# Pooled attention and a four-expert attention layer on one core: tail tokens of a batch, and of two batches, in one transfer each

## The chip, the cores and the metric

The kernel runs on one core of one Trainium2 chip. The metric is the device time of one execution in microseconds (us). Compute engines are PE (TensorE, matrix products into PSUM), ACT (ScalarE), DVE (VectorE) and POOL (GpSimd); SP (SyncE) issues the transfers, which 16 DMA engines carry out. Each engine works through its own instructions in order and waits at semaphores for the others.

## What is computed

The reference first pools k and v over runs of 8 tokens, attends with every q, and feeds the result as x to four attention experts; each token's result is weighted by a softmax over its two best experts.

```python
# q, k, v: (8 batches, 8 heads, 576 tokens, 64)
k_p = k.reshape(B, H, Sp, 8, D).mean(axis=3)          # Sp = 72
v_p = v.reshape(B, H, Sp, 8, D).mean(axis=3)
attn = softmax(q @ k_p^T / 8)
x = (attn @ v_p) as (B, 576, 512)
logits = x @ w_gate                                    # 4 experts, the best 2 kept
for e in range(4):
    q, k, v = x @ wq[e], x @ wk[e], x @ wv[e]          # 64 wide
    a = softmax(causal(q @ k^T / 8))
    out += weight[e] * (a @ v @ wo[e])                 # (B, 576, 512), zero weight if e isn't kept
```

## The kernel before

**Tiling.** A batch has 576 tokens: 512 "main" tokens, four rows of 128, and a tail of 64. The main tokens go batch by batch. Tails of q, x and out go by pairs of batches (b - 1, b) with b odd, 128 rows together (`part_t`, line 742). For k and v each batch's tail is loaded by itself (`load_tail`, line 308): a tile of 128 partitions by 4 heads by 64, whose lower 64 partitions hold the 64 tokens of heads 0 to 3, the upper 64 those of heads 4 to 7, by two transfers.

**Pooling on PE.** Sums over tokens are matrix products with 0 or 1/8 masks. `pm` (line 186) pools main tokens; `pmt` (lines 187 and 188) has two masks for tails: `pmt[0]` takes the lower 64 partitions to pooled tokens 64 to 71, `pmt[1]` the upper 64. `pool_k` (line 349) and `pool_v` (line 365) use mask 0 for heads 0 to 3 and mask 1 for heads 4 to 7.

**An order written out by hand.** The program is cut into units, named batch:unit. `ORDER` (line 21) lists them; a unit that yields stands there once for each of its stages. All instructions that the units issue keep the order of that list on their engine (`in_order`, line 125). The loop at line 955 walks the list. Units that matter here:

- `b:lk`, `b:lq`, `b:lv` load main tokens (`0:` in four parts, `1:` in two), `b:lkt`, `b:lvt`, `b:lqt` the tails, `b:kt` and `b:vt` cast the k and v tails on POOL; `b:kp`, `b:vp` pool.
- `b:q`, `b:s`, `b:a`, `b:x` are q transposed, pooled scores, scores times v, x transposed; `b:xd0` to `b:xd3` do the last by DMA transposes for batches 6 and 7.
- `b:p0` to `b:p3` and `b:v0`, `b:v2` project x; `b:c...` are the experts' scores (PE, then exponentials on ACT, then the causal mask on POOL); `b:o0`, `b:o1` scores times values (PE, then scaling on DVE); `b:t0`, `b:t1` transpose the result (by DMA for batches 4 to 6).
- `b:w0` ... and `b:y0` ... multiply 128 rows by wo: PE, then a copy to an `ofin` buffer, by ACT for w and by DVE for y, then a store of 128 rows on SP. There are four `ofin` buffers.
- `b:qx`, `sx`, `ax`, `xx`, `pt`, `vx`, `h0`, `h1`, `hd`, `ox`, `tx`, `w4` with b odd do the same for a pair's tails. The last, `wo` at line 926, computes 128 rows, copies them to an `ofin` buffer and stores them with two transfers of 64 rows, one for each batch. `7:w4` is the last unit of the kernel.
- `W:lk`, `W:lq`, `W:lv`, `W:lo` load weights, `W:c...` cast them, and `W:h0` to `W:h31` (`busy`, line 274) are fillers: two products of zeros each, which nothing reads.

A store's semaphore releases its `ofin` buffer; the copy that writes the buffer next waits for it.

Of the kernel before, what the change touches and what calls it, by code (L numbers as in the profile page):

```python
# [22 lines left out]
0:lk2 0:qc2a 1:q0 1:q1 0:qc0a W:h29 0:qc0d 1:q1 W:h1 0:lk0 W:h21 0:qc1d 0:qc1a 0:lk3 0:q0 0:lv0 W:h7
W:h3 0:qc3d 0:q0 0:ks2 0:q1 0:lk1 0:q1 0:lv2 W:h8 0:ks3 W:h19 W:h14 0:kp2 0:lvt 0:qc2d 0:lv3 0:ks0
0:q2 0:kp2 0:lv1 0:q2 1:kt W:h6 0:vs2 1:lq1 W:h2 0:kp3 0:ks1 W:h27 0:qc3a W:h18 0:q3 1:lk0 0:kp3
0:q3 0:kp1 0:s2 0:vs0 1:lk1 0:kp1 0:s1 0:vs3 0:vt 0:vs1 0:s3 0:kp0 W:h26 0:kp0 1:lv1 W:h15 0:vp 0:s1
0:s2 1:lvt W:h25 0:vp 1:lv0 W:h22 1:qc1a 0:s3 0:a2 1:qc1d 0:s0 W:h16 W:lk W:h24 0:a3 W:h5 0:lqt 0:a2
1:q2 1:ks0 W:h13 1:ks1 1:kp0 0:a3 1:q2 0:s0 0:a1 1:kp0 0:a0 W:h4 1:kp1 W:h28 1:q3 0:a0 1:kp1 0:a1
W:h17 1:s0 0:x0 1:s0 1:s2 1:q3 1:s3 0:x0 1:s1 W:lq W:lv 1:s2 1:lqt 1:vs1 0:x1 1:s3 2:lq W:h10 W:h9
0:x3 0:x1 1:vt W:h0 W:c1 0:x2 1:vs0 2:lkt 0:x3 2:lk W:c3 0:x2 1:vp 1:vp 0:p1 1:a0 1:a2 1:a2 1:s1  # L30
0:p1 W:c2 W:c0 0:p3 1:a1 1:qt 1:a0 2:qc 2:lv 1:a1 0:p3 0:p2 1:a3 W:cv 0:p0 0:p2 0:v2 0:p0 1:a3 2:kt
3:lqt 1:x2 0:v2 1:qx 0:c10 0:c10 0:c2 0:v0 2:lvt 1:qx 1:x3 1:x2 0:v0 0:c2 1:x0 1:x3 3:lk 0:c11 1:x0
1:sx 1:x1 1:x1 0:c11 0:c11 0:c00 0:c00 0:g1 0:g2 2:q3 2:q3 2:q0 1:sx 1:v2 0:c2 3:lvt 2:q2 0:c01 2:ks
2:lqt 0:c10 3:lkt 1:ax 2:q2 2:q1 2:q0 1:ax 1:p1 1:p1 1:v0 0:c01 2:kp 2:q1 1:v2 1:p2 2:vs 2:kp 0:g3
2:vt 1:v0 1:xx 2:s2 3:lq 1:xx 1:p2 2:s0 2:s1 1:vx 0:g4 2:s2 2:s1 1:vx 2:s0 3:lv 1:g1 2:s3 0:g5 1:g2
2:vp 0:o1 2:vp 2:s3 1:pt 2:a2 0:g6 3:ks 1:pt 3:kt 2:a0 1:p3 4:lq 3:qt 0:c01 0:o1 2:a3 2:a2 0:c00
1:p0 1:g3 2:a0 1:p3 2:a3 2:a1 1:c11 3:qc 3:kp 1:p0 4:lk 3:qx 3:vt 2:a1 1:hd 3:qx 1:c11 1:h0 1:hd
1:c2 3:kp 2:x2 2:x1 1:h0 2:x2 4:lkt 0:o0 2:x1 2:x3 4:lv 4:lvt 2:x0 1:c10 1:c2 1:g4 0:o0 3:sx 2:x3
1:c00 3:q1 2:x0 1:c2 1:c10 1:c00 3:q3 1:h1 3:q1 3:q3 3:q2 3:q0 2:v2 3:vs 1:h1 3:q2 1:c11 4:qc 3:q0
5:lq 0:t0 1:g5 0:t1 2:v0 2:v2 3:sx 3:s3 3:s1 0:t1 3:vp 0:t0 3:s3 2:p1 6:lvt 1:hd 4:ks 3:s1 2:p1 2:v0  # L40
3:s2 4:kt 1:c10 3:s0 3:vp 3:s2 3:a3 2:p0 3:a3 4:q2 3:a1 3:ax 4:q2 3:s0 4:q1 1:c01 2:p0 4:q3 4:q1
2:p3 1:c01 2:p3 5:lqt 2:c01 3:a1 4:q3 4:q0 3:ax 2:c01 3:a0 1:c00 4:q0 4:kp 4:kp 3:a2 3:a0 3:a2 2:p2
3:xx 2:p2 6:lkt 1:g6 4:s2 3:xx 4:s0 4:s0 5:lkt 4:s2 1:ox 3:x3 2:g1 1:c01 4:vt 1:o0 2:c00 4:s1 1:ox
3:x3 3:x1 4:vs 2:g2 2:c00 5:qc 4:vp 3:x1 4:s1 3:pt 4:s3 2:c11 3:pt 4:vp 1:o0 3:x0 3:x2 1:o1 2:c01
3:x0 W:lo 3:x2 5:q2 4:lqt 4:s3 2:c00 5:lk 2:c11 3:p3 5:q2 5:lvt 5:q3 1:o1 5:lv 2:c2 3:p3 2:c10 5:q1
4:a3 5:kt 2:c2 5:q3 2:c10 3:p1 4:a0 5:q1 3:p1 W:co 4:a3 3:p2 3:vx 4:a0 6:lqt 4:a1 3:p2 3:vx 3:v0
4:a1 7:lqt 3:v0 0:w0 2:g3 3:hd 6:lq 3:c10 2:c11 1:t1 4:a2 5:qt 2:g4 5:ks 0:w0 3:p0 1:t1 5:q0 4:a2
3:c10 3:hd 5:q0 5:vt 3:p0 3:h0 2:c2 3:c11 5:qx 5:kp 3:c11 3:v2 5:kp 5:qx 2:g5 0:w3 3:v2 3:h0 2:g6
4:x1 4:x1 5:s3 0:w3 3:g1 5:s1 4:x2 5:vs 1:t0 7:lkt 5:s3 2:c10 2:o0 6:lk 4:x2 0:w2 1:t0 4:x0 6:qc
2:o0 5:sx 5:s1 3:c2 3:c10 6:vt 0:w2 5:sx 5:s0 5:s0 7:kt 6:lv 3:c11 3:g2 4:x0 4:x3 5:vp 4:x3 3:c2  # L50
5:vp 3:hd 2:o1 4:p1 3:c2 2:o1 0:w1 4:p1 6:kt 5:s2 3:h1 0:w1 6:q3 6:q0 5:ax 6:q3 4:p0 6:q0 2:t0 3:h1
6:ks 5:ax 5:s2 3:g3 2:t0 0:w3 7:lvt 4:v2 2:t1 4:p0 6:q1 5:a2 3:g4 2:t1 7:qt 6:vs 5:a0 6:q1 5:a0 1:w3
4:p3 5:a1 1:w3 4:p3 5:a2 4:v2 4:p2 7:lq 5:xx 3:c00 3:c01 4:p2 5:a1 0:w2 6:kp 5:a3 3:c00 7:lk 5:xx
3:c01 6:kp 3:g5 3:g6 7:ks 0:w0 5:pt 6:q2 6:s3 5:a3 4:c01 6:q2 4:c00 5:pt 1:tx 1:tx 6:vp 5:x0 6:s3
4:v0 4:c00 5:x0 6:vp 2:w1 4:c01 4:v0 5:x3 6:s0 4:c2 2:w1 5:x1 5:x3 6:s1 5:x1 0:w1 6:s0 7:qc 6:s1
7:lv 2:w0 5:x2 3:o1 6:a0 5:x2 3:c01 2:w0 1:w4 3:c00 3:o1 5:p3 1:w4 4:c2 7:kp 6:a0 7:kp 4:g1 4:c10
4:c11 6:s2 5:p3 7:vs 4:c11 4:c10 7:q3 1:w4 3:ox 6:s2 7:q3 7:q2 5:v0 4:c10 3:ox 2:w1 6:a3 5:vx 7:q2
5:v0 2:w2 5:vx 6:a2 6:a1 6:a3 6:a2 1:w0 2:w2 1:w0 4:g2 2:w0 5:p2 2:w3 5:p2 5:hd 7:s3 6:a1 1:w0 7:q1
2:w3 5:hd 7:q1 4:c00 7:vt 4:c2 5:hd 5:v2 4:c11 4:g3 1:w2 3:t1 5:h1 7:s3 7:s1 1:w2 5:h1 7:s1 6:xd2
5:v2 2:w3 3:t1 7:vp 5:g1 5:p1 6:xd3 7:s2 4:g4 2:w2 7:vp 5:c10 5:p1 7:a3 7:s2 7:a3 7:q0 7:q0 4:g5  # L60
5:p0 3:o0 5:g2 4:c01 3:o0 7:qx 6:xd0 5:p0 4:o0 1:w1 5:c10 5:c2 7:s0 4:g6 7:qx 6:xd1 1:w1 3:t0 7:s0
6:p3 5:g3 3:t0 3:tx 3:tx 6:v2 6:p3 6:p0 5:c2 7:a1 1:w1 4:o0 7:a0 3:w4 6:v2 4:t0 7:a1 6:p0 1:w2 3:w4
6:p1 7:a2 5:g4 7:a0 3:w2 3:w2 5:h0 7:a2 5:c10 5:g5 7:sx 4:o1 6:p1 4:o1 1:w3 3:y1 3:y1 6:p2 5:c11
7:sx 5:h0 5:g6 5:c01 7:xd0 7:xd1 5:c11 6:p2 5:c01 5:c00 5:ox 6:v0 4:t1 3:w2 3:w3 5:ox 3:w3 3:w0 6:v0
3:w0 5:c01 7:ax 7:v0 7:ax 7:v0 4:w2 5:c11 7:xx 7:xd3 6:c2 5:c2 7:xx 6:g1 5:c00 3:y1 4:w2 6:c00 5:o1
4:w3 6:c2 7:xd2 5:o1 7:vx 3:w3 7:v2 3:w4 6:g2 6:c2 4:w3 7:p2 6:c11 6:c00 6:c10 6:g3 5:c00 7:v2 7:p2
6:c11 7:vx 6:c01 5:t1 7:p3 4:y1 6:g4 7:p3 4:w3 7:g1 4:y1 6:c10 4:y1 5:o0 5:o0 7:g2 6:c01 6:c00 6:g5
4:y0 4:y0 5:t0 7:p0 6:c11 6:c10 6:o1 7:c11 7:p0 6:g6 7:c10 6:c01 7:g3 7:g4 6:o1 4:w2 7:p1 5:tx 6:o0
5:tx 6:o0 7:c10 7:p1 7:c10 3:w0 7:c11 5:w4 5:y1 6:t1 7:g5 7:c2 7:c01 5:w4 7:c2 7:c00 7:c11 5:y1 4:y0
7:g6 5:y2 7:c01 7:pt 7:c2 7:c01 7:pt 5:y2 6:t0 7:c00 5:y1 5:y0 5:y0 7:c00 7:o1 5:w3 7:o1 7:hd 6:y1  # L70
# [919 lines left out]
```

## Time and profile before

| | us |
|---|---|
| three runs | 177.66, 178.21, 178.53 |
| their median | 178.21 |
| the profiled execution | 176.43 |
| its span, first to last instruction | 174.7 |

The span was taken at a granted TensorE clock of 0.996 of full speed. The profile's page gives busy time and shares of the span for each engine, a picture of the span in 40 slices, and the chain of work that ended last, followed back from the last instruction: at each step to what released it, or to the instruction before it on its engine. Rows of groups read: line, engine, operation, out<-in, shapes, how many | busy time, mean ns of one | idle time just before them and what ended it. L133 is the line of the helper that records every ordered instruction, so most rows are told apart by their tiles. Rows of a timeline read: start, length, engine, line, operation, and in brackets the idle time before it with its releaser. SPq is SP's queue of transfers, where the length is that of the issue alone; the rows of DMA issues give KB of one transfer and the median time from issue to landing.

| DMA, 40 slices of 4.37 us | |
|---|---|
| busy share in tenths | 4999999999999999979999999061632866267886 |

Of 42.03 MB in all, 30.42 MB are read from HBM and 9.44 MB written to it. 36 stores leave from `ofin`: 28 of 256 KB and 8 of 128 KB; the last copy into such a buffer starts at 170.3 us and the last issue at 171.4 us.

### The profile page before, as it was taken

What the parts mean: (1) busy time and instruction counts of PE and PEld (TensorE: products, weight loads), DVE (VectorE), ACT (ScalarE), POOL (GpSimd) and SP (SyncE); (2) the same over time, 40 slices, a digit from 0 to 9 for tenths busy, and PEclk for the clock granted to TensorE, in tenths of its full rate; (3) what the DMA queues carried; (4) which work ended last, traced back from release to release, by engine and by line L of the source; (5) the groups of instructions that cost most, each with busy time, mean ns of one, the idle gap of its engine ahead of it and who ended that gap; (6) DMA issues with size and microseconds to landing.
All of it is one profiled execution on the core that took longest, in us unless ns stands there. A gap on an engine that the chain in (4) does not pass through costs nothing.

```text
span 174.7 us, 5295 instructions
## 1 busy us (share of the span) xinstructions
PE 163.1 (93%) x2088; PEld 101.2 (58%) x2088; DVE 123.7 (71%) x354; ACT 125.0 (72%) x176; POOL 101.2 (58%) x227
## 2 busy tenths in 40 slices
PE   7698999999999999999999999999999999989990
PEld 2244454567577745775675757675466586546550
DVE  6456586777688867988877697689678656675760
ACT  2210909876788977789899859896987877888841
POOL 8504333147989999873689995963802054655200
PEclk9999999999999999999999999999999999999998
DMA  4999999999999999979999999061632866267886
GB/s 151 280 337 304 344 296 282 263 325 262 250 221 345 346 281 288 190 209 311 260 284 339 332 365 365 25 177 67 172 72 90 183 181 157 90 135 250 267 332 194
DMA packets 52968, 42.03 MB, mean 241 GB/s; under 512 B 21968, under 2 KB 48080, under 8 KB 52944
## 3 DMA queue, kind: packets, MB, share of 16 engines
q1 hardware_dynamic: 52944, 41.70, 86.4%
q8 instruction: 16, 0.26, 0.7%
q14 instruction: 8, 0.07, 0.1%
HBM read 30.42 MB, written 9.44 MB: 228 GB/s over the span
## 4 chain that ended last, share of the span: by engine, by line
PE 72%; DMA 11%; ACT 8%; DVE 4%; SPq 1%; issue 1%; ACTq 0%; DVEq 0%
PE p_ps L133 15%; PE v_ps L133 7%; PE y_ps L133 6%; PE idle_ps L133 5%; PE sB_ps L133 5%; PE sA_ps L133 4%; PE oA_ps L133 4%; PE qT_ps L133 4%; PE oB_ps L133 4%; PE vp_ps L133 3%; DMA out_dram<-ofin 3%; DMA ktail<-in_k_dram 3%; PE xT_ps L133 3%; DMA kraw<-in_k_dram 3%; PE oBt_ps L133 3%; ACT etA L133 3%
## 5 line engine op out<-in xcount | busy, mean ns | idle before, releaser
L133 ACT ACTIVATE etA<-sA_ps 72x1024 bf16<-72x1024 f32 x32 | 31.4, 1018 | 12.7 <-PE sA_ps L133 12.6
L133 ACT ACTIVATE etB<-sB_ps 128x1024 bf16<-128x1024 f32 x32 | 32.3, 1027 | 3.0 <-PE sB_ps L133 2.7
L133 PE MATMUL p_ps<-xT,wqk 128*128 128x512 bf16 x128 | 32.9, 379 | 0.1
L133 POOL TENSOR_SCALAR_AFFINE_SELECT etB<-etB 128x256 bf16<-128x256 bf16 x48 | 18.5, 407 | 12.0 <-ACT etB L133 11.8
L133 ACT CAST qk<-p_ps 128x512 bf16<-128x512 f32 x32 | 18.8, 587 | 9.2 <-PE p_ps L133 9.0
L133 DVE TENSOR_TENSOR x_tm<-oA_ps,rzA 128x512 bf16<-128x512 f32 x32 | 22.1, 691 | 1.1
L133 POOL TENSOR_TENSOR vsum<-vraw 128x512 bf16<-128x512 f32 (+2 forms) x18 | 18.4, 1043 | 7.5 <-DMA vraw<-in_v_dram 7.5
L133 PE MATMUL idle_ps<-idle 128*128 128x512 bf16 x64 | 19.6, 418 | 1.9 <-DVE idle L160 1.2
L133 PEld LDWEIGHTS <-wqk 128*128 128x128 bf16 x192 | 15.0, 97 | 10.3 <-issue 0.9
L133 POOL TENSOR_TENSOR ksum<-kraw 128x512 bf16<-128x512 f32 (+1 forms) x16 | 17.8, 1134 | 4.8 <-DMA kraw<-in_k_dram 4.6
L133 PE MATMUL y_ps<-wo_t,oT 128*128 128x512 bf16 x64 | 18.4, 379 | 1.0 <-DMA oT<-o_sc 0.7
L133 DVE COPY qT<-qT_ps 128x512 bf16<-128x512 bf16 x32 | 15.2, 486 | 5.8 <-PE qT_ps L133 5.5
L133 ACT COPY ofin<-y_ps 128x512 f32<-128x512 f32 x20 | 11.7, 586 | 10.0 <-PE y_ps L133 6.8
L133 PE MATMUL v_ps<-wvg,xT 128*128 128x260 bf16 x128 | 17.0, 274 | 0.0
L133 PE MATMUL qT_ps<-ident,qbf 128*128 128x128 bf16 x128 | 11.9, 220 | 2.1 <-DVE qbf L133 1.4
L133 PE MATMUL sB_ps<-qk 64*128 64x256 bf16 (+3 forms) x128 | 13.6, 299 | 0.0
L133 DVE COPY xT<-xT_ps 128x512 bf16<-128x512 bf16 x24 | 9.7, 419 | 4.6 <-PE xT_ps L133 4.5
L133 PEld LDWEIGHTS <-xT 128*128 128x128 bf16 x128 | 11.6, 97 | 2.4 <-DVE x_tt L133 0.4
L133 POOL CAST qbf<-qraw 128x2048 bf16<-128x2048 f32 x6 | 11.3, 1889 | 2.8 <-PE sB_ps L133 2.4
L133 PEld LDWEIGHTS <-etA 72*128 72x128 bf16 x256 | 10.6, 97 | 3.9 <-issue 1.0
L133 PEld LDWEIGHTS <-qbf 128*128 128x128 bf16 x128 | 8.3, 97 | 7.4 <-issue 2.7
L133 PEld LDWEIGHTS <-etB 128*128 128x128 bf16 x256 | 11.4, 97 | 1.7 <-POOL etB L133 0.5
(123 smaller groups left out, 333.1 us busy)
## 6 DMA issues: line engine op xcount, KB each, us to landing
out_dram<-ofin SPq DMA_DIRECT2D x28, 256.0 KB, 2.7
qraw<-in_q_dram SPq DMA_DIRECT2D x6, 1024.0 KB, 9.5
...
qraw<-in_q_dram SPq DMA_DIRECT2D x4, 256.0 KB, 4.7
...
ktail<-in_k_dram SPq DMA_DIRECT2D x16, 64.0 KB, 5.7
kraw<-in_k_dram SPq DMA_DIRECT2D x4, 256.0 KB, 4.8
```

The costliest lines, as they stand in the source:

```text
L133: return tc.keep_in_program_order(fn(*args, **kwargs))
```

## The change

Four things change.

1. The tails of k and of v of a batch come in one transfer of 128 KB each. The tile has the same shape, but its rows are laid out otherwise: partition 2t + half holds token t, of heads 0 to 3 for half 0 and of heads 4 to 7 for half 1.
2. The two tail masks follow that layout. POOL makes one mask `pmr`, in which 16 partitions in a row belong to one pooled token; DVE reduces the identity to two columns that say whether a partition is even or odd, and multiplies.
3. `part_t`'s `wo` stores its 128 rows with one transfer for both batches. For the last pair its copy is split in two halves of 256 columns, one on ACT, one on DVE.
4. `ORDER` is a new list of the same units, each the same number of times.

```diff
 ORDER = """
-0:lq0 W:h12 1:lq0 0:lkt W:h20 0:lq2 0:lq3 W:h30 0:kt 1:qc0a W:h23 1:lkt W:h11 1:qc0d 0:lq1 1:q0
...
+0:lq2 W:h30 0:qc2d 0:lq1 W:h16 W:h8 0:qc1a W:h12 0:qc1d W:h9 W:h13 0:lq0 0:qc2a 0:lv0 0:lk3 W:h17
...
+6:p1 5:hd 7:a2 7:a0 5:h0 3:w4 1:w1 5:c2 7:xd1 2:w3 3:t0 4:o1 7:sx 6:p2 3:t0 5:h0 5:c11 6:p2 1:w0
+5:c01 7:xd2 5:c01 4:o1 5:c00 3:y1 5:ox 5:c11 7:ax 4:t1 3:y1 3:w2 5:c00 3:w2 5:c00 7:ax 6:v0 5:c11
+6:v2 5:ox 3:w0 3:w0 6:v0 6:c00 6:v2 6:c2 7:xd3 6:g1 7:xd0 7:xx 4:w3 5:o1 7:xx 6:c00 3:w0 6:g2 7:vx
+5:c01 7:v2 3:w4 7:vx 6:c2 4:w3 3:w2 7:v0 7:v2 4:w2 5:o1 6:g3 4:w2 7:p2 3:y1 7:v0 7:p2 3:w3 6:c10
+6:c11 6:g4 3:w3 6:c01 6:c10 4:y1 7:p3 6:c10 6:c11 4:y1 5:o0 7:p3 7:p0 4:w2 6:c01 4:y0 3:w3 7:c11
+6:c11 7:c10 7:p0 5:o0 6:c00 5:tx 5:t1 4:y1 7:c10 4:y0 6:c2 6:g5 6:c01 6:o1 7:g1 7:c11 5:t0 4:y0 7:p1
+5:tx 6:o0 6:g6 5:w4 7:g2 4:w3 7:p1 7:c2 7:g3 6:o1 5:w4 6:o0 7:c11 6:t1 7:c00 5:y1 5:y2 7:c2 6:t0
+5:y1 7:c10 5:y2 7:c2 7:g4 7:c01 7:pt 5:y0 7:c01 7:c01 5:w4 7:pt 7:o1 7:g5 5:y1 5:w3 7:c00 5:y0 5:w3
+7:g6 7:hd 7:c00 7:o1 6:y1 7:hd 7:o0 6:y1 6:w0 7:t1 7:h1 5:y2 7:h0 7:o0 7:t1 6:w0 7:hd 7:t0 5:w3 6:y3
+7:t0 6:y1 6:w0 7:h1 5:y0 6:y3 7:z2 7:h0 6:w2 6:y3 7:ox 7:z2 7:z0 6:w2 7:ox 7:tx 6:w2 7:tx W:h31 7:z0
+7:w4 7:w4 7:w4
 """
...
-    pmt = [pooling("pmt0", MAIN, POOLW), pooling("pmt1", MAIN - 64, POOLW)]
-    nc.gpsimd.memset(pmt[1][0:64, :], 0.0)
+    rows = pooling("pmr", 2 * MAIN, 2 * POOLW)
+    parity = const.tile([128, 2, 1], BF16, name="parity")
+    nc.vector.tensor_reduce(
+        out=parity[:, :, 0], in_=ident[:, :].rearrange("p (i half) -> p half i", half=2),
+        axis=AX_X, op=MAXOP,
+    )
+    pmt = []
+    for half in range(2):
+        t = const.tile([128, 128], BF16, name=f"pmt{half}")
+        nc.vector.tensor_tensor(
+            out=t[:], in0=rows[:], in1=parity[:, half, :].to_broadcast([128, 128]), op=MULT
+        )
+        pmt.append(t)
...
-            for half in range(2):
-                sp.dma_start(
-                    out=t[half * 64 : half * 64 + 64, :].rearrange("p (h d) -> p h d", h=4),
-                    in_=srcs[nm][b, half * 4 : half * 4 + 4, MAIN:S, :].rearrange("h t d -> t h d"),
-                )
+            sp.dma_start(
+                out=t[:].rearrange("p (h d) -> p h d", h=4),
+                in_=srcs[nm][b, :, MAIN:S, :].rearrange("h t d -> t h d"),
+            )
...
-            copy(out=t[:], in_=ps[:])
-            yield
-            for i, b_ in enumerate(both):
-                store(out[b_, MAIN:S, :], t[i * TAIL : (i + 1) * TAIL, :])
+            if b < B - 1:
+                copy(out=t[:], in_=ps[:])
+            else:
+                for half, eng in ((slice(0, DM // 2), act.copy), (slice(DM // 2, DM), dve.tensor_copy)):
+                    eng(out=t[:, half], in_=ps[:, half])
+            yield
+            store(out[b - 1 : b + 1, MAIN:S, :], t[:])
```

More of the change, by code (lines that the diff above doesn't have):

```diff
@@ L21 @@
 ORDER = """
-0:lq0 W:h12 1:lq0 0:lkt W:h20 0:lq2 0:lq3 W:h30 0:kt 1:qc0a W:h23 1:lkt W:h11 1:qc0d 0:lq1 1:q0
[L23 to L70, printed above, removed]
@@ L71 @@
-7:o0 5:w3 6:w0 5:y2 5:y0 6:y1 7:hd 7:o0 7:h1 7:t1 6:w0 7:h0 7:t0 7:t1 7:t0 7:h1 7:hd 5:w3 5:w4 6:y3
-6:w0 6:y1 6:y3 6:y3 7:h0 7:z2 7:ox 6:w2 7:z2 7:z0 7:ox 7:tx 6:w2 7:tx 6:w2 W:h31 7:w4 7:z0 7:w4 7:w4
+0:lq2 W:h30 0:qc2d 0:lq1 W:h16 W:h8 0:qc1a W:h12 0:qc1d W:h9 W:h13 0:lq0 0:qc2a 0:lv0 0:lk3 W:h17
+W:h2 W:h23 0:ks3 0:q1 0:lq3 W:h6 0:lkt W:h1 0:kt 0:lk1 W:h19 W:h7 0:lv1 0:qc3a 0:vs0 0:lv2 0:lk2
+0:q1 1:lq0 W:h3 0:q2 W:h11 0:q2 0:ks1 W:h15 0:qc0d W:h4 0:lv3 W:h24 0:kp3 0:kp1 0:kp1 0:qc3d 0:ks2
@@ new lines @@
+0:kp2 0:qc0a 0:s1 0:lk0 0:kp2 0:kp3 0:q3 0:q3 0:lvt 1:qc0d 1:lq1 0:q0 1:qc0a W:h20 0:q0 1:lk1 1:q0
+0:s1 0:vs2 0:ks0 0:vs1 W:h29 0:vs3 1:lkt 0:kp0 1:lvt 0:s3 0:s2 1:qc1a 1:lk0 1:q0 0:vt 0:s2 0:kp0
+1:qc1d 0:vp 0:s0 0:vp W:h27 1:q2 1:lv0 1:q2 1:ks1 0:s3 W:h21 0:a1 0:a1 1:lv1 1:q1 1:vt 0:a2 W:lk
+W:h0 0:a3 W:lq W:h5 1:q3 1:q1 W:h25 1:kt 1:ks0 W:h22 W:lv 1:vs0 0:a2 0:lqt W:h14 1:lqt 0:a3 1:kp1
+0:s0 0:a0 1:q3 1:kp1 0:a0 1:kp0 1:s2 1:s3 0:x0 1:kp0 0:x2 0:x0 0:x2 1:s1 1:s2 2:lq 1:s0 W:h10 0:x1
+W:h18 1:s1 2:lk W:h26 1:vs1 1:s0 W:c1 0:x1 0:x3 2:lkt W:c3 1:s3 1:vp 2:lv 0:x3 1:vp 0:p1 W:c0 1:a3
@@ new lines @@
+1:a2 0:p3 2:lvt W:c2 3:lk 1:a0 1:qt 1:a2 0:p1 2:qc 1:a3 0:p3 0:p0 W:cv 1:a0 1:a1 1:a1 0:p2 0:p0 0:v0
+0:p2 1:qx 0:v2 1:x0 2:lqt 1:qx 0:v0 1:x0 0:c11 0:c2 W:h28 1:x1 0:v2 1:x3 0:c2 0:g1 0:c11 1:x1 0:c00
+0:c2 1:sx 1:x2 3:lqt 1:sx 1:x3 0:g2 1:x2 2:q1 0:c00 3:lkt 2:q1 3:lq 0:c10 0:c10 1:p1 1:ax 0:c11
+3:lvt 1:v2 0:g3 2:ks 2:q0 3:lv 4:lq 1:ax 1:v2 0:c01 1:p1 2:q3 2:kt 2:q0 0:g4 2:vs 2:q3 0:g5 1:v0
+2:kp 1:p2 2:vt 2:kp 1:xx 0:c01 4:lk 1:v0 0:g6 4:lkt 0:c10 2:s0 2:s3 1:p2 0:c00 1:xx 2:q2 4:lvt 2:s0
+2:s3 2:q2 1:vx 2:s1 1:vx 2:s2 1:g1 2:vp 2:vp 0:o1 2:s2 2:s1 3:ks 4:lv 1:pt 3:kt 2:a3 2:a1 0:o1 2:a2
@@ new lines @@
+0:c01 2:a3 1:pt 1:p3 2:a1 1:p0 2:a2 1:p3 2:a0 2:a0 1:c11 3:kp 1:p0 3:qt 3:qx 1:g2 1:c11 3:kp 1:hd
+1:h0 3:qx 1:c2 1:hd 1:g3 2:x2 2:x1 0:o0 2:x2 1:h0 2:x1 2:x3 3:qc 0:o0 2:x3 1:c2 2:x0 2:x0 1:c10
+1:c00 3:sx 1:c10 3:q2 3:q3 3:q3 3:sx 3:q2 1:hd 2:v2 1:c00 0:t1 3:s3 3:q1 0:t1 1:c11 2:v2 3:q0 5:lq
+2:v0 3:q1 3:s3 0:t0 3:q0 1:h1 3:vt 3:vs 2:v0 0:t0 3:s1 3:vp 1:h1 3:vp 2:g1 1:g4 5:lk 2:p1 3:s0 3:s2
+3:s1 4:qc 1:c10 3:a3 1:c00 4:ks 3:a3 4:q2 4:q2 2:p1 2:p0 1:c01 3:s0 4:q1 4:kt 3:s2 3:a1 4:vt 2:p0
+3:ax 1:c01 4:q1 1:c01 4:q3 2:p3 2:g2 1:c2 3:a2 3:a1 4:q3 3:ax 4:q0 2:c01 2:p3 4:kp 3:a0 4:q0 1:g5
@@ new lines @@
+2:c01 2:p2 4:kp 2:p2 3:a2 3:xx 4:s0 2:c00 4:lqt 1:ox 1:g6 3:a0 3:xx 3:x1 5:lqt 1:o0 2:c00 4:vs 4:s2
+4:s0 5:lkt 4:s1 1:ox 3:x3 3:x1 4:s2 3:x3 5:qc 4:s1 4:vp 3:pt 3:pt 4:vp 2:c11 2:c11 W:lo 4:s3 6:lkt
+3:x2 1:o0 5:lvt 3:x0 3:x2 1:o1 5:q2 3:x0 3:p3 4:s3 5:q2 5:q3 2:c2 1:o1 3:p3 5:lv 5:q3 2:g3 2:c10
+2:c2 5:q1 4:a3 2:g4 2:c01 3:p2 2:c10 5:qt 5:q1 4:a1 4:a3 3:p2 4:a1 5:ks W:co 3:p1 2:g5 4:a0 2:c10
+3:v0 6:lq 0:w0 3:p1 3:vx 4:a0 0:w0 5:kt 3:hd 2:c2 3:c10 7:lqt 3:v0 4:a2 6:lvt 2:c11 3:vx 2:g6 3:hd
+1:t1 1:t1 3:p0 4:a2 5:q0 3:c10 3:c11 3:p0 3:c11 3:h0 5:q0 2:c00 5:qx 5:qx 5:vs 5:kp 5:kp 3:v2 0:w3
@@ new lines @@
+3:h0 5:vt 4:x1 5:s1 0:w3 3:v2 4:x1 5:s3 1:t0 4:x2 2:o0 6:qc 6:lv 1:t0 6:vt 4:x0 5:s1 4:x2 5:s3 0:w2
+3:c10 5:sx 0:w2 3:c11 2:o0 3:c2 5:sx 5:s0 4:x3 6:lk 4:x0 4:x3 5:vp 7:lkt 0:w1 3:c2 2:o1 5:vp 3:g1
+6:kt 6:q3 0:w2 0:w1 5:s0 5:ax 6:q3 2:o1 3:g2 4:p1 2:t0 3:h1 3:g3 4:p1 7:lk 5:s2 2:t0 6:q0 3:h1 6:q0
+4:p0 6:q1 5:ax 5:s2 6:q1 4:v2 3:hd 2:t1 3:g4 7:kt 4:v2 4:p0 5:a0 5:a2 7:lq 1:w3 5:a1 0:w1 2:t1 5:a0
+5:a2 1:w3 4:p3 4:p2 4:p3 6:ks 6:vs 5:xx 3:c01 5:a1 4:p2 3:c00 6:kp 5:xx 5:a3 5:pt 3:c01 3:c2 3:c00
@@ new lines @@
+6:kp 6:q2 3:g5 6:s3 4:c01 5:pt 6:s3 3:c01 5:a3 4:c00 1:tx 6:q2 6:vp 1:tx 5:x0 4:v0 5:x0 6:vp 2:w1
+4:c01 6:lqt 4:c00 5:x3 6:s1 2:w1 3:g6 7:qc 4:v0 6:s0 5:x3 6:s0 0:w0 5:x2 4:g1 5:x2 6:s1 5:x1 3:o1
+5:x1 1:w4 1:w3 7:lv 1:w4 2:w0 7:ks 6:a0 4:c2 2:w0 3:o1 4:c01 6:s2 6:a0 7:kp 5:p3 7:kp 4:c2 7:q3 0:w3
+5:p3 4:c11 4:c10 7:q3 4:g2 6:s2 7:lvt 2:w0 7:q2 3:ox 7:q2 4:c10 2:w2 6:a1 5:v0 3:ox 2:w2 6:a1 7:vt
+5:v0 5:vx 5:vx 7:qt 6:a3 5:p2 6:a2 1:w0 6:a3 5:hd 4:c11 7:s3 5:p2 6:a2 1:w0 4:c00 2:w3 7:s3 2:w1
+2:w3 7:q1 7:q1 4:c2 1:w4 5:v2 7:vs 6:xd3 1:w2 4:g3 4:g4 3:t1 5:v2 3:c00 4:c11 5:g1 6:xd0 5:hd 7:s1
@@ new lines @@
+1:w2 5:c10 7:s1 3:t1 7:s2 7:s2 7:vp 5:p1 5:h1 7:vp 5:g2 5:p1 6:xd1 7:q0 7:a3 5:p0 6:xd2 7:q0 5:h1
+4:g5 3:tx 7:a3 4:c10 5:p0 3:tx 3:o0 1:w1 7:qx 5:g3 4:o0 5:c10 5:c2 4:g6 3:o0 7:s0 7:qx 4:o0 2:w2
+6:p3 1:w1 7:a1 5:c2 7:s0 5:g4 6:p0 5:c10 5:g5 7:a2 7:a1 7:a0 1:w2 5:g6 6:p3 6:p1 6:p0 3:w4 7:sx 4:t0
+6:p1 5:hd 7:a2 7:a0 5:h0 3:w4 1:w1 5:c2 7:xd1 2:w3 3:t0 4:o1 7:sx 6:p2 3:t0 5:h0 5:c11 6:p2 1:w0
+5:c01 7:xd2 5:c01 4:o1 5:c00 3:y1 5:ox 5:c11 7:ax 4:t1 3:y1 3:w2 5:c00 3:w2 5:c00 7:ax 6:v0 5:c11
+6:v2 5:ox 3:w0 3:w0 6:v0 6:c00 6:v2 6:c2 7:xd3 6:g1 7:xd0 7:xx 4:w3 5:o1 7:xx 6:c00 3:w0 6:g2 7:vx
```

## The prediction

> **What bounds the kernel now.** I read the page first (busy shares, the chain by engine), then a table of stretches, then the end of the chain of waits.
>
> ```profile
> PE 163.1 (93%) x2088; PEld 101.2 (58%) x2088; DVE 123.7 (71%) x354; ACT 125.0 (72%) x176; POOL 101.2 (58%) x227
> PE 72%; DMA 11%; ACT 8%; DVE 4%; SPq 1%; issue 1%; ACTq 0%; DVEq 0%
> ```
> ```profile
> 20.00:30.00 10.00, 9.52 (x96) 4.96 (x95) 7.37 (x18) 5.08 (x7) 4.91 (x7) 1.00 1.13 302
> 31.00:90.00 59.00, 57.92 (x823) 39.13 (x821) 45.75 (x133) 47.70 (x67) 43.76 (x79) 1.00 1.07 275
> 90.00:130.00 40.00, 39.76 (x561) 26.08 (x560) 31.53 (x91) 33.53 (x48) 29.51 (x57) 1.00 0.72 219
> 130.00:170.90 40.90, 38.76 (x522) 23.39 (x518) 27.12 (x79) 31.57 (x47) 14.40 (x47) 1.00 0.64 184
> ```
>
> Columns: stretch, its length, busy time of PE, PEld, DVE, ACT, POOL, granted clock, DMA share, GB/s. Before 31 us the sixteen DMA engines are full (share 1.13) and PE fills its time with filler matmuls; from 31 to 130 us PE is busy 97.7 of 99 us; from 130 us there are holes, 2.1 us in 41. So loads set the time up to 31 us, PE from there, and the end is what follows PE's last matmul:
>
> ```profile
> 159.99 2.23 DMA out_dram<-ofin
> 162.31 0.59 ACT ofin L133
> 162.90 0.27 ACT etD L133
> 164.76 0.40 PE oT_ps L133 x4
> 169.64 0.57 PE yt_ps L133 x2
> 170.28 0.59 ACT ofin L133
> ```
>
> In the last 15 us the chain already runs once through a store: ACT may not copy into an `ofin` buffer until the store that last read it has landed. Landing times of stores are therefore a price on the path, not only at the very end.
>
> **What each part costs.**
>
> *Tail loads of k and v.* 32 issues become 16.
>
> ```profile
> ktail<-in_k_dram SPq DMA_DIRECT2D x16, 64.0 KB, 5.7
> vtail<-in_v_dram SPq DMA_DIRECT2D x16, 64.0 KB, 7.1
> qtail<-in_q_dram SPq DMA_DIRECT2D x8, 128.0 KB, 7.1
> 1.79 1.41 SPq L133 DMA_DIRECT2D ktail<-in_k_dram  x2
> ```
>
> The q tail already moves 128 KB in one transfer and lands in 7.1 us, no later than the v halves. A pair costs SP 1.41 us to issue, one transfer about half. From 0 to 31 us SP is ahead of full DMA engines, afterwards PE hides the loads: 0 to -0.7 us, I take -0.2.
>
> *Masks.* POOL builds one mask fewer (2.35 us for two selects alone), DVE gets a reduce and two products of 128x128, by the nearest row, the 0.25 us copy of `perm`, about 0.8 us.
>
> ```profile
> 2.59 2.35 POOL L176 TENSOR_SCALAR_AFFINE_SELECT pmt<-pmt 128x72 bf16<-128x72 bf16 x2
> 4.48 0.25 DVE L166 COPY perm<-ident 128x128 bf16<-128x128 bf16 x1
> 6.60 0.43 DVE L133 CAST qbf<-qraw 128x512 bf16<-128x512 f32 x1 [1.63 <-DMA qraw<-in_q_dram]
> 12.91 0.20 PE L133 MATMUL kpT_ps<-pmt,ktb 128*128 128x72 bf16 x1
> ```
>
> DVE idles 1.63 us before its first cast, waiting for q, and the masks are first used at 12.91 us: 0. Without that cover it would be 0.8 us.
>
> *Order.* The two orders hold the same units. I counted the PE units that stand ahead of the first projection `0:p1`: the same set in both, except that one filler, `W:h28`, moves from ahead of it to after it. All loads of batches 0 and 1 but their q tails stand ahead of `W:lk` in both, so the DMA-bound start stays. One pair of fillers costs
>
> ```profile
> 22.60 0.59 PE L133 MATMUL idle_ps<-idle 128*128 128x512 bf16 x2
> ```
>
> 0.59 us where PE is full, 0 in a hole: +0.3. What else the order moves I can bound by PE's holes alone: about 3.5 us idle between 31 and 170.9 us (139.9 less the three stretches' 136.4) is all that a perfect order could win; as much could be lost. I take 0 and keep ±1.5.
>
> *Last copy split.* A half copy:
>
> ```profile
> 8.11 0.71 ACT L133 CAST qbf<-qraw 128x256 bf16<-128x256 f32 x2 [0.90 <-DMA qraw<-in_q_dram]
> 168.39 0.42 DVE L133 TENSOR_TENSOR o_st<-oBt_ps,gt 128x256 bf16<-128x256 f32 x1
> ```
>
> 0.36 us on ACT, 0.42 on DVE, side by side, for 0.59: -0.2.
>
> *Joint tail store.* This is the term that decides.
>
> ```profile
> 171.00:172.00 1.00, 0.00 (x0) 0.00 (x0) 0.00 (x0) 0.00 (x0) 0.00 (x0) 1.00 0.97 367
> 172.00:173.00 1.00, 0.00 (x0) 0.00 (x0) 0.00 (x0) 0.00 (x0) 0.00 (x0) 1.00 0.97 217
> ```
> ```profile
> DMA packets 384, 0.66 MB, mean 170 GB/s; under 512 B 64, under 2 KB 64, under 8 KB 384
> q1 hardware_dynamic: 384, 0.66, 58.1%
> out_dram<-ofin SPq DMA_DIRECT2D x2, 128.0 KB, 2.3
> ```
> ```profile
> 170.90 1.11 SPq L133 DMA_DIRECT2D out_dram<-ofin  x2
> out_dram<-ofin SPq DMA_DIRECT2D x28, 256.0 KB, 2.7
> ```
>
> The first two rows are the drain at the end, the next three its DMA from 170.95 us on. A second with 128-row stores moves 367 GB/s, the next, with the two 64-row stores, 217 GB/s, both with the engines 0.97 busy: how a transfer's rows lie sets its rate. At 367 GB/s each of 16 engines moves a 2 KB row in 0.97 x 16 x 2.048 / 367 = 0.087 us. The 64 small packets are 16 for each of four stores that end in this stretch: every store so far ran on all 16 engines. All have 64 or 128 rows outermost on both sides. The joint store does not: its rows in `out` are two runs of 64, one per batch, 576 rows apart, so that side is [2, 64, 512] with 2 outermost.
>
> If it is still spread over 16 engines, a store costs 8 x 0.087 = 0.7 us of engine time, and the pair's second issue (half of 1.11 us) goes too. If it is split along the outermost count, two engines get 64 rows each: 64 x 0.087 = 5.6 us, and it lands 4.9 us later, 2.4 + 4.9 = 7.3 us after its issue. No row of this trace shows a transfer with fewer than 16 in that place. I take two engines: that a transfer's rate goes by its outermost rows is what the 64-row stores show, and an outermost count of 2 gives two parts.
>
> The Trainium skill (DMA: Bandwidth & Descriptors, Why a DMA increments its semaphore by 16 and not by 1) says the engine count is the largest number up to 16 that divides both sides' slowest dimension, here 2. The same page's Rules for kernel authors ask for one 128-partition transfer in place of two halves, which by 367 against 217 GB/s this trace agrees with; by that alone the change would be a gain at the end.
>
> On two engines the four joint stores cost as follows; distances are unit counts of the new order priced by these pieces of the chain and groups:
>
> ```profile
> 146.99 0.45 PE vt_ps L133 x4
> 147.44 0.94 PE v_ps L133 x8
> 149.24 0.76 PE sB_ps L133 x10
> 150.97 0.43 PE y_ps L133 x2
> 151.40 0.61 PE oB_ps L133 x20
> ```
> ```profile
> 158.67 1.22 SPq L133 DMA_TRANSPOSE oT<-o_sc  x1
> 163.57 0.20 DVE L133 RECIPROCAL oB_ps<-oB_ps 128x8 f32<-128x8 f32 x1
> 164.01 0.69 DVE L133 TENSOR_TENSOR o_sc<-oB_ps,gt 128x512 bf16<-128x512 f32 x1
> L133 ACT ACTIVATE etB<-sB_ps 128x1024 bf16<-128x1024 f32 x32 | 32.3, 1027 | 3.0 <-PE sB_ps L133 2.7
> 162.31 0.59 ACT L133 COPY ofin<-y_ps 128x512 f32<-128x512 f32 x1 [0.71 <-DMA out_dram<-ofin]
> ```
>
> Which buffer a copy gets I took as the one whose store was issued first among those free (four `ofin` buffers).
>
> - `1:w4`: the next copy into its buffer is `1:w2`, and SP reaches the store as soon as `2:w0` is copied, two dozen units and, priced by the same pieces, some 12 us of PE earlier: 0.
> - `3:w4`: its store follows `3:w0`'s, so it issues about 1.2 us after that copy starts and lands at 1.2 + 7.3 = 8.5. The buffer's next writer is ACT's `4:w2`, behind 6:c00, 6:c2, 7:xx, 4:w3, 5:o1, 7:vx, 7:v2, 7:v0 and itself: 0.76 + 0.40 + 0.43 + 0.61 + 0.45 + 2 x 0.94 + 0.43 = 5.0 us. ACT waits 3.5 us, and behind it its exponentials. PE has a projection and the second PSUM buffer to go on with; between 0 and 3.5 I take 1.5.
> - `5:w4`: its store stands behind the DMA transposes 6:t1 and 6:t0. The matmuls of 6:o0 end 0.43 us before those of `5:w4`; DVE's scaling takes from 163.57 to 164.70, 1.1 us; 6:t0's issue 1.22 us, and 6:t1's may still run for 0.5: so the store issues some 2.4 us after its own copy starts and lands at 9.7. The buffer's next writer is `5:w3`, with three exponentials and one cast ahead of it on ACT: 0.59 + 3 x 1.03 + 0.59 = 4.3 us. ACT waits 5.4 us, where 0.71 us was waited before, so at most 4.7 more; queued behind it are 7:hd, 7:h1 and 7:h0, which PE needs for its last scores-times-values, so little hides it: +4.0 (the other bound is 0, if other buffers come free first).
> - `7:w4`: nothing is behind it. Its second store issued at 170.90 + 0.55 and landed 2.3 us later, at 173.8; from there to the end of the span are 0.9 us. Now: issue at 170.7 (the split's 0.2 earlier), landing 178.0, end 178.9: +4.2, the split included.
>
> Sum, in the order named: 1.5 + 4.0 + 4.2 for the stores, -0.2 loads, +0.3 filler, 0 masks: +9.8 us on a span of 174.7, to 184.5. The profiled execution took 176.43 us, 1.7 more than its span; the shown runs have a median of 178.21, 1.8 above that. On the median: 188.0.
>
> **Rivals.**
>
> 1. *Two engines, but only the end pays.* The waits at `3:w4` and `5:w4` are taken up by ACT's idle time or another buffer. For it: ACT is busy 31.57 of 40.9 us there. Against it: the chain shows an ACT copy that waited for a store in this very place. 178.2 + 4.2 + 0.1 = 182.5.
> 2. *Sixteen engines* (the other side). The spread does not go by the outermost count of `out`; then the end gains the split (0.2), the second issue (0.5) and the slower drain of the half stores. It decides in the packets: eight 2 KB rows per engine, or 64. 0.2 + 0.5 + 0.2 of loads - 0.3 filler: 177.6; without the filler's cost 177.3.
> 3. *The new order itself loses* on sixteen engines: PE-bound stages run the filler at 0.59 us and get about 1 us more holes than the 3.5 they have, the drain gains nothing, the split and the loads 0.4: 178.2 + 0.6 + 1.0 - 0.4 = 179.4.
>
> **How the numbers follow.** Forecast 0.50, rival 1 0.32, rival 2 0.13, rival 3 0.05. Around the forecast the `3:w4` and `5:w4` terms run from 0 to 3.5 and 0 to 4.7 and the order ±1.5, so 184 to 192; rival 1 with the order's ±1.5 reaches down to 181.0. The range 181.0 to 192.0 leaves out rivals 2 and 3 and a little above. A change under 0.5% (0.9 us) can't be told from none: faster, most of rival 2, 0.10; same, the rest of it and part of rival 3, 0.06; slower 0.84.
>
> **What will show it.** The DMA issues: 256 KB `ofin` stores, four of them landing 7 us after issue (two engines) or 2.4 (sixteen). After the last ACT and DVE half copies, DMA share near 2/16 = 0.125 and some 46 GB/s for over 4 us. A wait of ACT for `out_dram<-ofin` of 3 to 5 us before two copies, with PE idle behind the second. Masks: DVE's first qbf cast not later than 6.6 us. If the last store lands in about 2.4 us, the forecast is wrong at its first step; if it lands in 7 but ACT waits under 1 us, rival 1 holds.

## The result, and the profile after

| | before | after |
|---|---|---|
| median of four runs, us | 178.03 (177.66 to 178.53) | 192.09 (191.14 to 192.52) |
| ratio to before | | 1.078, 95% interval 1.073 to 1.083 |
| profiled execution: span, us | 174.7 | 190.2 |
| granted TensorE clock over the span | 0.996 | 0.943 |

The change costs 14 us; the forecast was 10. The forecast time was 188.0 us in a range of 181.0 to 192.0: 192.09 us lies at the upper end, 0.1 us past it. From the page of the changed kernel, the busy times, the granted clock in 40 slices of 4.75 us, and the row of the 256 KB stores:

```profile
PE 165.0 (87%) x2088; PEld 101.9 (54%) x2088; DVE 123.5 (65%) x358; ACT 124.8 (66%) x176; POOL 100.1 (53%) x222
PEclk9999999999999999999999999999999579975965
out_dram<-ofin SPq DMA_DIRECT2D x32, 256.0 KB, 2.4
```

No engine has more to do (the same 2088 matmuls take 1.9 us more). The median landing time in that row, 2.4 us, says nothing of the four joint stores: the trace has no landing time for them in that row. The table of stretches shows where the time stands, and the first new thing: the clock column (after the five busy times) falls.

```profile
130.00:140.00 10.00, 10.00 (x168) 6.74 (x166) 6.69 (x19) 7.72 (x11) 1.69 (x5) 1.00 0.70 147
140.00:150.00 10.00, 5.75 (x59) 3.64 (x59) 4.33 (x16) 3.13 (x5) 2.25 (x9) 0.90 0.53 114
150.00:160.00 10.00, 9.17 (x95) 4.45 (x95) 4.18 (x15) 7.60 (x11) 3.94 (x12) 0.76 0.48 111
160.00:170.00 10.00, 6.46 (x89) 3.59 (x86) 4.29 (x11) 4.58 (x7) 4.10 (x13) 0.93 0.61 147
170.00:180.00 10.00, 7.79 (x95) 4.37 (x95) 5.16 (x13) 5.42 (x9) 0.77 (x2) 0.73 0.58 213
```

PE stands still for 4.3 us of the stretch from 140 and 3.5 us of that from 160. The waits (us in total, times, longest) and ACT's timeline at the two places:

```profile
ACT ofin L134 <- DMA out_dram<-ofin: 13.5, 4, 6.1
PE y_ps L134 <- ACT ofin L134: 10.5, 2, 5.4
DVE ofin L134 <- DMA out_dram<-ofin: 5.9, 1, 5.9
```
```profile
144.09 0.58 ACT L134 COPY ofin<-y_ps 128x512 f32<-128x512 f32 x1 [1.53 <-DMA out_dram<-ofin]
150.20 0.58 ACT L134 COPY ofin<-y_ps 128x512 f32<-128x512 f32 x1 [5.41 <-DMA out_dram<-ofin]
171.50 0.58 ACT L134 COPY ofin<-y_ps 128x512 f32<-128x512 f32 x1 [6.10 <-DMA out_dram<-ofin]
```

150.20 is `4:w2`, 171.50 is `5:w3`: the copies that the prediction named. The chain of waits runs through the second, and through the last pair's half copies:

```profile
163.49 7.91 DMA out_dram<-ofin
...
171.50 0.59 ACT ofin L134
...
179.82 0.57 PE yt_ps L134 x2
...
180.46 0.38 ACT ofin L134
...
180.86 0.42 DVE ofin L134
```

The joint store of `5:w4` takes 7.91 us from issue to landing. In the trace's records of semaphore updates an ordinary 128-row store has 16 updates. Each of the four joint stores has three: one about 1 us after its issue, and two late ones, the last of them after 8.04 us (`1:w4`), 7.86 (`3:w4`), 7.91 (`5:w4`) and 7.84 (`7:w4`). DVE's wait of 5.9 us, in front of a copy at 172.1 us, is for an ordinary store that was issued behind the joint one, at 164.1 us, and landed 7.9 us later. The last joint store is the drain of the kernel: issued at 181.3 us, and alone in these seconds (clock, then DMA share, then GB/s at the row's end):

```profile
185.00:186.00 1.00, 0.00 (x0) 0.00 (x0) 0.00 (x0) 0.00 (x0) 0.00 (x0) 0.50 0.13 45
186.00:187.00 1.00, 0.00 (x0) 0.00 (x0) 0.00 (x0) 0.00 (x0) 0.00 (x0) 0.50 0.14 53
187.00:188.00 1.00, 0.00 (x0) 0.00 (x0) 0.00 (x0) 0.00 (x0) 0.00 (x0) 0.50 0.13 49
```

A share of 0.13 is two engines of sixteen, at 45 to 53 GB/s where the old drain moved 367. From the last matmul to the end were 4.5 us before (170.2 to 174.7) and are 9.8 now (180.4 to 190.2).

### The profile page after: what moved, and what is told of

Read it like the earlier page. It is cut to its first block, busy times and chain, and to the rows that moved or that the text cites. A ratio compares the mean times of both kernels' runs of the same rounds, so it can differ in the third digit from the quotient of the medians.

```text
span 190.2 us, 5256 instructions
## 1 busy us (share of the span) xinstructions
PE 165.0 (87%) x2088; PEld 101.9 (54%) x2088; DVE 123.5 (65%) x358; ACT 124.8 (66%) x176; POOL 100.1 (53%) x222
## 4 chain that ended last, share of the span: by engine, by line
PE 64%; DMA 14%; ACT 8%; DVE 4%; SPq 3%; issue 1%; ACTq 0%; DVEq 0%
PE p_ps L134 13%; DMA out_dram<-ofin 10%; PE y_ps L134 6%; PE v_ps L134 5%; PE sB_ps L134 5%; PE idle_ps L134 4%; PE oA_ps L134 4%; PE qT_ps L134 4%; PE sA_ps L134 4%; SPq L134 3%; DMA kraw<-in_k_dram 3%; PE oB_ps L134 3%; ACT etA L134 3%; PE xT_ps L134 3%; PE oBt_ps L134 2%; PE vp_ps L134 2%
## 5 line engine op out<-in xcount | busy, mean ns | idle before, releaser
L134 PE MATMUL y_ps<-wo_t,oT 128*128 128x512 bf16 x64 | 19.8, 406 | 10.7 <-ACT ofin L134 10.5
L134 PE MATMUL idle_ps<-idle 128*128 128x512 bf16 x64 | 18.8, 411 | 2.2 <-DVE idle L161 1.2
L134 DVE COPY ofin<-y_ps 128x512 f32<-128x512 f32 x8 | 5.4, 690 | 16.1 <-PE y_ps L134 10.1
L134 PE MATMUL sB_ps<-qk 64*128 64x512 bf16 (+3 forms) x128 | 14.2, 313 | 0.5 <-ACT etC L134 0.5
L134 PEld LDWEIGHTS <-oT 128*128 128x128 bf16 x64 | 5.3, 100 | 14.9 <-issue 11.8
L134 PE MATMUL oA_ps<-vp,etA 72*128 72x65 bf16 x256 | 12.5, 194 | 0.2 <-ACT etA L134 0.2
L134 PE MATMUL oB_ps<-vaug,etB 128*128 128x65 bf16 x256 | 12.4, 194 | 0.0
```

What stands on the lines that cost most here:

```text
L134: return tc.keep_in_program_order(fn(*args, **kwargs))
```

## The experiments

Ratios are to the kernel before, run beside each experiment on the same chip. Its median there was 177.08, 178.07 or 178.12 us, so parts are compared by ratios, times 178.03.

**No joint store.**

```diff
-            store(out[b - 1 : b + 1, MAIN:S, :], t[:])
+            for i, b_ in enumerate(both):
+                store(out[b_, MAIN:S, :], t[i * TAIL : (i + 1) * TAIL, :])
```

> The changed kernel with the old pair of 64-row stores, all else as changed. Theory (the joint store runs on two engines, lands about 7.8 us after its issue, and holds its buffer that long): the whole loss goes, 177 to 178.7, no wait of ACT for an ofin store above 1.5 us. Rival (the new order, the masks or the merged loads lose): it stays above 185.

174.03 us, ratio 0.9825 (0.9772 to 0.9877): 3.0 to 4.7 us under the time expected. The loss is all in the joint stores, and what is left of the change is a gain of 1.75%, which the forecast did not have. ACT's longest wait for a store:

```profile
ACT ofin L134 <- DMA out_dram<-ofin: 1.7, 3, 0.7
```

**The new order alone**, on the kernel before (only the `ORDER` string is exchanged).

> The kernel before with the new order alone. Theory: the order by itself is worth little, 177 to 179.5. Rival (the order loses by itself): above 183.

174.39 us, ratio 0.9846 (0.9791 to 0.9901): the order alone gains 2.7 us, and the time lies under the 177 to 179.5 expected. First and last start of the projections, by tile (duration min/median/max, first to last), before and then with the new order:

```profile
L133 PE MATMUL p_ps<-xT,wqk x128: 376/379/389, 31.0 to 155.0; 128*128 128x512 bf16 x128
```
```profile
L134 PE MATMUL p_ps<-xT,wqk x114: 376/379/390, 30.5 to 153.4; 128*128 128x512 bf16 x114
```

The first projection starts 0.5 us earlier, the last 1.6 us: in these two traces most of the gain lies after 31 us. That it was won in holes of PE is not shown, since only 114 of the 128 records are in the second trace, and PE's idle time can't be compared.

**Loads, masks and split alone**: the run with no joint store, with the old `ORDER`.

> Old order, separate tail stores; merged loads of k and v tails, masks and the split of the last copy as changed. Theory (these parts are worth little): 0.2 to 1.2 us under the kernel before. Rival (DVE's new mask work delays the start): slower than before.

176.67 us, ratio 0.9923 (0.9899 to 0.9946): 1.4 us, a little more than expected; which of the three parts it is was not measured. DVE's mask work does not delay the kernel. In the changed kernel it lies among the memsets and the first casts, and the first cast starts at 5.03 us, before the 6.6 us of the prediction's sign:

```profile
4.56 0.27 DVE L191 TENSOR_REDUCE parity<-ident 128x2 bf16<-128x128 bf16 x1
...
5.03 0.23 DVE L134 CAST qbf<-qraw 128x256 bf16<-128x256 f32 x1
5.39 0.49 DVE L198 TENSOR_TENSOR pmt<-pmr,parity 128x128 bf16<-128x128 bf16 x2
```

**One joint store at a time.** The changed kernel with the joint store under one condition, `b == 7`, `b == 3`, `b == 5` or `b == 1`, and two stores for the other pairs:

```diff
+            if b == 7:
                 store(out[b - 1 : b + 1, MAIN:S, :], t[:])
+            else:
+                for i, b_ in enumerate(both):
+                    store(out[b_, MAIN:S, :], t[i * TAIL : (i + 1) * TAIL, :])
```

> Joint store for the last pair alone, 64-row stores for the other three pairs, all else as changed. Theory: only the end is paid, about 5 us over the run with no joint store, 182 to 184, and the two waits of ACT (5.4 and 6.1 us) are gone. Rival (the waits come from the new order, which leaves too little room between a store and the next copy whatever its length): the waits stay at 4 us or more and the time is 187 or more.

> Joint store for the pair of batches 2 and 3 alone. Theory: one wait of ACT of some 5 us for an ofin store about 25 us ahead of the end and a part of it lost to the time: 177 to 180. Rival (only stores near the end pay, later work makes it good): 174 to 175.

> Joint store for the pair of batches 4 and 5 alone. Theory: the wait of ACT of about 6 us before 5:w3 is all on the path: 179 to 181. Rival (ACT's idle time takes it up): 174 to 176.

> Joint store for the first pair alone. Theory (nobody wants its buffer before it lands, and its two engines have nothing urgent behind it): 173.7 to 174.7, as with none. Rival (the DMA transposes of batch 6 stand behind it on the two engines and PE waits for x): 176 or more.

| joint store of | us | ratio (interval) | over the run with none, us |
|---|---|---|---|
| `7:w4` | 179.94 | 1.0163 (1.0097 to 1.0230) | 6.0 |
| `3:w4` | 181.09 | 1.0171 (1.0134 to 1.0209) | 6.2 |
| `5:w4` | 180.61 | 1.0146 (1.0089 to 1.0202) | 5.7 |
| `1:w4` | 174.26 | 0.9806 (0.9766 to 0.9845) | -0.3 |

The last column is the difference of the ratios, to 0.9825, times 178.03. The four add up to 17.6 us, all four together cost (1.078 - 0.9825) x 178.03 = 17.0: they hardly overlap. `1:w4` is free, as expected, though its store lands after 8 us too: nobody waits for it. `7:w4` came out 2 us under the expected time only because the run with none did; its loss is the expected 5 and one more. `3:w4` came out 1 us above the expected times; `5:w4` came out as expected. With `7:w4` alone ACT waits at most 1.2 us for a store, so the new order by itself doesn't make the two long waits.

**Joint stores in the old order**: the kernel before, with only its two tail stores replaced by the joint one.

> The kernel before with the joint stores alone, old order. Theory: the stores land after 7 to 8 us in this order too; the old order has some 9 us between the store of 3:w4 and the next copy into its buffer, so no wait there, and stores 5:w4 late, so that its rows and the last store's queue up on the same two engines: 184 to 187, less than the 192 of the full change. Rival (only the end pays, the waits belong to the order): 182 to 183.5.

190.96 us without its slowest run of 193.88, ratio 1.0791 (1.0706 to 1.0876): the expectation failed, by 4 us, and so did its rival. The chain runs through three landings of 8 us, one of each joint store ahead of the last, in an order that was to leave room:

```profile
114.07 7.95 DMA out_dram<-ofin
122.12 0.59 ACT ofin L133
...
150.23 8.64 DMA out_dram<-ofin
158.95 0.70 DVE ofin L133
...
170.97 7.66 DMA out_dram<-ofin
178.73 0.59 ACT ofin L133
```

Each time it is the next copy into the joint store's own buffer that waits, 3.7 to 3.9 us (in total, times, longest):

```profile
ACT ofin L133 <- DMA out_dram<-ofin: 7.6, 2, 3.9
DVE ofin L133 <- DMA out_dram<-ofin: 3.7, 1, 3.7
```

So the engines came to these copies 4 to 5 us after the joint store's issue (for `3:w4` 5.0 us, where the expectation counted some 9), and the buffer of `1:w4`, which the expectation left out, was wanted early as well.

**Memory of its own.** To part the wait for the buffer from the queue behind the store, the run with `5:w4` joint was repeated with the rows of that store in a free `kraw` tile in place of an `ofin` buffer:

```diff
+            if b == 5:
+                own = rawp.tile([128, H, NR * D], FP32, name="kraw", tag="kraw")
+                t = own[:, 0:2, :].rearrange("p h n -> p (h n)")
+            else:
                 t = ofp.tile([128, DM], FP32, name="ofin", tag="ofin")
```

> As the run with the joint store for batches 4 and 5 alone, but its rows lie in memory of their own, not in one of the four ofin buffers. Theory (the copy waits for the buffer): the 6 us wait before 5:w3 goes; the stores behind it still end late on the two engines, so a shorter wait comes at 6:y1 or 6:w0: 175.5 to 179. Rival (the two engines' queue alone sets the loss): as the run beside it, 179 to 181.

179.84 us, ratio 1.0107 (1.0070 to 1.0144) against 1.0146 (1.0089 to 1.0202): the intervals overlap, and the rival holds. ACT no longer waits for a store ahead of `5:w3`. But DVE still does (4.75 us, against 5.9 us in the run beside it), for an ordinary store of 128 rows that was issued after the joint one, at 157.0 us (timeline of DVE, then that store's landing time by tile):

```profile
164.47 0.69 DVE L134 COPY ofin<-y_ps 128x512 f32<-128x512 f32 x1 [4.75 <-DMA out_dram<-ofin]
```
```profile
L134 SPq DMA_DIRECT2D out_dram<-ofin x1: 362/362/362, 157.0 to 157.0; - x1
...
DMA to landing us min/median/max: 7.4/7.4/7.4
```

An ordinary store lands after 7.4 us too when it stands behind a joint one. In the trace 14 of its 16 semaphore updates come 2.3 to 3.5 us after its issue and the last two after 7.2 and 7.4: two of its shares came late, when the joint store was done. The slow transfer slows what is queued behind it.

**The same joint stores, rows interleaved.** The transfer keeps its 256 KB and its two far regions of `out`; only the order of its rows changes, so that 64 and not 2 is outermost in `out`:

```diff
-            dve.tensor_copy(out=st["oT"][:], in_=ps[:])
+            dve.tensor_copy(
+                out=st["oT"][:].rearrange("p e (t i) -> p e i t", i=2),
+                in_=ps[:].rearrange("p e (i t) -> p e i t", i=2),
+            )
...
-            store(out[b - 1 : b + 1, MAIN:S, :], t[:])
+            store(out[b - 1 : b + 1, MAIN:S, :].rearrange("b t n -> t b n"), t[:])
```

> The changed kernel with its four joint stores, but the 128 rows interleaved (row 2t + batch), by a permuted copy of oTt, so that the store's side in out is [64, 2, 512] and no longer [2, 64, 512]. Theory (the split along the outermost count costs, not the joining): every joint store lands in about 2.4 us and the time is 173 to 174.5, as with separate stores or a little under. Rival (one transfer over two far regions is slow as such): it stays above 188.

173.18 us, ratio 0.9724 (0.9687 to 0.9761): the lowest time of all, 10% under the change as made. Its last store, by tile:

```profile
L134 SPq DMA_DIRECT2D out_dram<-ofin x1: 550/550/550, 168.4 to 168.4; - x1
...
DMA to landing us min/median/max: 2.4/2.4/2.4
```

All four joint stores now have 16 semaphore updates and land after 2.4 to 2.5 us. So neither the joining nor the two far regions cost anything; the outermost count of 2 does.

**A hole filled.** The run with `3:w4` joint, with fillers where PE stood still in it:

```diff
-5:c01 7:v2 3:w4 7:vx 6:c2 4:w3 3:w2 7:v0 7:v2 4:w2 5:o1 6:g3 4:w2 7:p2 3:y1 7:v0 7:p2 3:w3 6:c10
+5:c01 7:v2 3:w4 7:vx 6:c2 4:w3 3:w2 7:v0 7:v2 4:w2 5:o1 6:g3 4:w2 7:p2 3:y1 7:v0 7:p2 W:fill 3:w3 6:c10
...
+    def fill():
+        ps = ps2.tile([128, 2, 512], FP32, name="fill_ps", tag="ps2")
+        for _ in range(24):
+            pe.matmul(out=ps[:, 0, :], lhsT=idle[:, 0:128], rhs=idle[:], start=True, stop=True)
+
+    units["W:fill"] = fill
```

> As the run with the joint store for batches 2 and 3 alone (181.1 us, 7.1 over the run with none, of which PE's hole behind ACT's wait is 4.8), with 24 filler products, some 5 us, ahead of 3:w3, where PE stands still in that run. Theory (the rest, 2.3 us, is the granted clock, which falls to 0.5 after the hole): the clock stays at 1.0 and the time falls to 178 to 179.5. Rival (the rest is work that came late, the clock only follows): 181 or more.

179.40 us against 181.09, ratio 1.0090 (1.0055 to 1.0125) against 1.0171 (1.0134 to 1.0209); the intervals do not meet. Without and then with the fillers (PE's busy time is the second number, the clock the third from the end):

```profile
146.00:148.00 2.00, 0.00 (x0) 0.00 (x0) 0.04 (x1) 0.00 (x0) 0.00 (x0) 1.00 0.57 114
148.00:150.00 2.00, 0.00 (x0) 0.00 (x0) 0.00 (x0) 0.18 (x1) 0.00 (x0) 0.56 0.13 49
150.00:152.00 2.00, 1.54 (x6) 0.39 (x7) 0.00 (x0) 1.39 (x3) 0.00 (x0) 0.50 0.39 142
152.00:154.00 2.00, 2.00 (x13) 0.69 (x8) 0.13 (x1) 1.99 (x3) 0.41 (x1) 0.50 0.49 158
```
```profile
148.00:150.00 2.00, 2.00 (x12) 0.88 (x10) 0.00 (x0) 0.06 (x1) 0.00 (x0) 1.00 0.13 49
150.00:152.00 2.00, 2.00 (x17) 0.85 (x15) 0.00 (x0) 1.52 (x4) 0.00 (x0) 1.00 0.36 134
152.00:154.00 2.00, 2.00 (x28) 1.15 (x25) 0.69 (x1) 2.00 (x4) 0.42 (x2) 1.00 0.53 171
```

ACT waits as long in both (5.45 and 5.43 us). Work that nobody reads makes the kernel 1.4 us faster by the ratios (1.7 by the times), because the real work after it runs at the full clock. The first two matmuls behind the hole take 1.01 us without the fillers and 0.59 us with them, though they start 0.4 us later:

```profile
150.46 1.01 PE L134 MATMUL y_ps<-wo_t,oT 128*128 128x512 bf16 x2 [4.75 <-ACT ofin L134]
150.86 0.59 PE L134 MATMUL y_ps<-wo_t,oT 128*128 128x512 bf16 x2
```

**The filler `W:h28` back ahead of the first projection**, on the interleaved version (the unit is moved in `ORDER` to stand behind `W:h26`).

> As the interleaved version (173.18 us), with the filler W:h28 back ahead of the first projection. Theory (it costs 0.5 us where PE is full): 172.5 to 172.9. Rival (it stands in a hole): 173.1 to 173.7.

173.83 us, ratio 0.9781 (0.9755 to 0.9808), against 0.9724 (0.9687 to 0.9761): no gain, so the theory failed and the rival holds. No cost of the filler shows where the new order has it.

## Why the prediction was right, point by point, and where its sizes were off

*Two engines.* Right. The drain shows two engines' share, the stores land after 7.8 to 8.0 us where 7.3 were predicted, and with interleaved rows after 2.4. The Trainium skill (DMA: Bandwidth & Descriptors, Why a DMA increments its semaphore by 16 and not by 1) gives the rule, the largest number up to 16 that divides both sides' slowest dimension; with [2, 64, 512] and [64, 2, 512] in `out` this case's trace agrees with it on both sides. The same page's advice to use one 128-partition transfer in place of two halves holds in the interleaved version and not in the change as made: the other side's outermost count decides.

*Which copies wait.* Right: `1:w4` nobody, `3:w4` ACT at `4:w2`, `5:w4` ACT at `5:w3`. But the reason was half of it. The prediction let a wait hang on the buffer; the run with memory of its own shows that the queue on the two engines holds the ordinary stores behind it as well, so moving one buffer away gains little: the joint store of `5:w4` still costs (1.0107 - 0.9825) x 178.03 = 5.0 us. In the old order all three waits were for the joint stores' own buffers; what failed there was the count of the time until the next copy.

*Sizes.* In us of the median:

| term | predicted | measured |
|---|---|---|
| `3:w4` | 1.5 | 6.2 |
| `5:w4` | 4.0 | 5.7 |
| `7:w4`, with the split | 4.2 | 6.0, the split not in it |
| order | 0.3 | -2.7 |
| loads and masks; measured with the split | -0.2 | -1.4 |
| whole change | 9.8 | 14.1 |

The measured rows for the parts come from kernels that differ by one part each, and add up to 13.8. The order and the other parts were also measured together, in the run with no joint store: 3.1 us and not 2.7 + 1.4 = 4.1, a difference within the intervals.

- `3:w4` was the mis-sized term. The prediction had ACT waiting 3.5 us and let PE work through more than half of it. ACT waited 5.4 us: counted from the start of the copy of `3:w0` at 140.13 us, the store was issued after 2.1 us (predicted 1.2), took 7.9 us to land (7.3), and ACT was free after 4.7 us (5.0). And PE waited 4.8 us of it in the run with this store alone, because it soon needed the PSUM buffer that the copy holds:

```profile
PE y_ps L134 <- ACT ofin L134: 5.3, 2, 4.8
```

  The rest, 1.4 us by the filled hole, is the clock, which the prediction did not price at all.
- `5:w4`: the wait was 6.1 us (predicted 5.4), and the clock is at 0.73 in the ten us after 170. How much of its 5.7 us the clock is was not measured by itself.
- `7:w4`: the profiles of the run with this store alone and the run with none differ by 5.1 us from the last matmul to the end (178.1 - 168.3 against 172.0 - 167.3), 0.7 more than 4.2 and the split's 0.2; the store landed 0.5 us later than predicted. The other 0.9 us lie ahead of the last matmul and were not followed up.
- The order won 2.7 us, more than the 1.5 that were kept as its bound. The prediction's 3.5 us of holes would have allowed it, though 0.7 us of these lie behind PE's last matmul, which ends at 170.2 us. Which of the moved units win the time stays open; the one edit that was priced, `W:h28`, shows no cost.

The two errors have opposite signs: the joint stores cost 17.0 us and not 9.7, the rest of the change gains 3.1 us and does not merely break even. That the sum came within 4.3 us is in part luck: with the stores mis-sized alone, the change would have cost some 17 us. Rival 1 (only the end pays) and rival 2 (sixteen engines) fell with the first profile; rival 2's time is what the change would have been with interleaved rows, and better: 173.2, not 177.6. Rival 3 fell with the order alone.
